# Attention and two mixture layers on one core: a static order planned with later transfers, and one batch's gate logits moved from TensorE to VectorE

## The chip, the cores and the metric

The kernel runs on one core of one Trainium2 chip. A core has five engines that run their own instruction streams and meet at semaphores: TensorE (PE, matmuls; PEld is its weight load), VectorE (DVE), ScalarE (ACT), GpSimd (POOL), and SyncE (SP), which here issues nearly all transfers. The metric is the device time of one execution in microseconds. The kernel before takes 978.87 us, the median of 3 runs (978.06 to 982.78).

## The reference

What is computed, cut to what matters:

```python
def _attn_ref(q, k, v, f):                      # batch 4, heads 8, sequence 576, head size 64
    scores = scale * np.matmul(q, k.transpose(0, 1, 3, 2))
    cum = np.cumsum(np.log(np.clip(f, 0.0001, 1.0)), axis=-1)
    decay = cum[:, :, :, None] - cum[:, :, None, :]
    scores = np.where(causal, -1e9, scores + decay)
    ...                                          # softmax over keys, times v
def _moe_ref(x, w_in, w_out):                    # 2304 tokens, 512 -> 2048 -> 512
    h = np.maximum(x @ w_in, 0.0)
    return h * h @ w_out
def _moe2_ref(x, w_gate, w1, w2):                # 8 experts, 512 -> 1024 -> 512
    cap = N // E                                 # 288 tokens for each expert
    logits = x @ w_gate
    order = np.argsort(-logits.flatten())
    ...                                          # greedy: best pair of token and expert first, while
    ...                                          # the token is free and the expert has room
    for e in range(E):
        mask = assigned == e
        out[mask] = np.maximum(x[mask] @ w1[e], 0.0) @ w2[e]
```

The three stages follow one another: attention gives x, the dense layer gives a new x (called x2 here), and the last layer sends each token of x2 to one expert. The gate's logits are compared exactly, so x2 has to be precise: each matmul of the dense layer is done as three products of high and low parts.

## The kernel before, in words

**The order.** Nothing runs in the order in which the code is written. The code records tasks (class `Sched`, method `op`): what a task reads and writes, which engines can do it (`alts`, with a cost in ns for each), and a priority (`s.base` at the time of recording, then the sequence). `run` then plays all tasks through a list scheduler in its own time: at each moment every free engine takes the ready task of the lowest priority number for which it finds buffers. A task that follows another becomes ready after a latency of the engines involved (`LAT`). For a transfer the plan counts 450 ns of issue, 650 ns of start, its bytes at 310 GB/s on one shared queue, and then 900 ns until it has landed. The result is a fixed order for each engine, and the choice of engine for each task. On the chip each engine takes its instructions strictly in that order and waits in front of one whose inputs are late.

**Attention** works by pairs of heads, four pairs for each of four batches (`pair`, `att_tail`). Queries and keys come by transfers (qk), and the decay of a head comes as a `row` of 128 x 576, a transfer from the scratch `cumd` in DRAM. A mask is added to the row's diagonal block (L512, GpSimd or VectorE), TensorE makes scores (L500), VectorE adds row and scores and takes the minimum in one instruction (L517, statistics in `st`), ScalarE takes the exponential (L524), TensorE transposes it (L556), ScalarE or VectorE copies it out of PSUM (`pa`, `pb`), and TensorE multiplies by v (L573). For the normalisation the sums of a pair get an epsilon (L603) and a reciprocal (L604), are transposed (L606), written to the scratch `rd`, and read back broadcast into the buffer `wraw` (four transfers); the product with them is L622. The result goes to the scratch `xd`.

**Weights of the dense layer** arrive as 64-bit numbers of 512 KB a piece (`w_piece`, into buffers z). VectorE makes 32-bit floats of them in three steps (L652, L653, L654, buffer `wa` or z), ScalarE or GpSimd rounds to the high part (helper lines L384, L386), GpSimd or VectorE subtracts for the low part (L656). The 32 pieces are spread over the attention stage.

**The dense layer** goes by chunks of 256 tokens (`moe1_chunk`): L692 to L694 up, ReLU, square, rounding, low part (L709), L716 to L718 down. As soon as a batch of attention is done its chunks are mixed into the rest of attention.

**The logits** are made in three ways. For batches in `DL` (1 and 2) VectorE multiplies the tile of x2 by each expert's gate column and sums, eight instructions per tile of 128 tokens (`x2_sums`, L797), with the gate columns broadcast in `wgb`. For batch 0, and for one chunk of batch 3, `x2_tail` has TensorE transpose the tile (L822) and multiply by the gate (L830, two passes for 32-bit floats). For the last two chunks of the dense layer the gate is multiplied into w_out beforehand: `gate_weights` does that with 128 instructions like those sums (L852) as filler on VectorE, and TensorE's L758 and L759 use the result. All logits have to be there before routing starts.

**Routing and experts** follow (`phase`, `expert`): routing of expert m overlaps with the matmuls of the experts before it.

Of the kernel before, what the change touches and what calls it, by code (L numbers as in the profile page):

```python
# [8 lines left out]
F = mybir.dt.float32  # L9
R = mybir.dt.float32r  # L10
BF = mybir.dt.bfloat16
# [3 lines left out]
OP = mybir.AluOpType  # L15
# [4 lines left out]
B, H, S, D = 4, 8, 576, 64  # L20
# [5 lines left out]
WHI, WLO = "act pool", "dve pool"  # L26
# [10 lines left out]
HV = [0]  # L37
NSM = 4

DL = (1, 2)  # L40
ABASE = (0, 0.5, 0.6, 2)
HM = 50.0
LM = 40.0
# [24 lines left out]
    "pool": {"pool": 96.0, "dve": 130.0, "act": 130.0, "pe": 230.0, "sp": 150.0},  # L68
}
DMA_GBS = 310.0  # L70
SLOT_LAT = 180.0


# [21 lines left out]


class Task:
    __slots__ = ("alts", "fn", "prio", "deps", "succ", "ready", "bufs", "done", "start", "eng", "nbytes", "seq")


class Sched:
# [31 lines left out]
                o.succ.append(t)  # L133
        return t

    def op(self, alts, fn, r=(), w=(), nbytes=0, prio=None, after=None):
        t = Task()
        t.alts = alts
        t.fn = fn
        t.seq = len(self.tasks)  # L140
        t.prio = (self.base if prio is None else prio, t.seq)
        t.deps, t.succ, t.ready, t.done, t.start, t.eng = set(), [], 0.0, None, None, None
        t.nbytes = nbytes
        t.bufs = []
        if after is not None:
            t.deps.add(after)
        for lst, wr in ((r, False), (w, True)):
            for x in lst:
                b, key = x if isinstance(x, tuple) else (x, None)
                if b not in t.bufs:  # L150
                    t.bufs.append(b)
                    b.left += 1
                    if b.after is not None:
                        t.deps.add(b.after)
                for o, k in b.writers:
                    if o is not t and (k is None or key is None or k == key):
                        t.deps.add(o)
                if wr:
                    for o, k in b.readers:
                        if o is not t and (k is None or key is None or k == key):  # L160
                            t.deps.add(o)
                    b.writers.append((t, key))
                else:
                    b.readers.append((t, key))
        for o in t.deps:
            o.succ.append(t)
        self.tasks.append(t)
        return t

    def run(self):  # L170
# [42 lines left out]
        while ndone < len(self.tasks):  # L213
            progress = True
            while progress:
                progress = False
                for e in list(cand):
                    if busy.get(e, 0.0) > now:
                        continue
                    h = cand[e]  # L220
                    skipped = []
                    pick = None
                    while h:
                        p, t = heapq.heappop(h)
                        if t in started:
                            continue
                        r = t.ready.get(e, 0.0) if isinstance(t.ready, dict) else t.ready
                        if r > now:
                            skipped.append((p, t))
                            continue  # L230
                        sl = can_alloc(t)
                        if sl is None:
                            skipped.append((p, t))
                            continue
                        pick = t
                        break
                    for x in skipped:
                        heapq.heappush(h, x)
                    if pick is None:
                        continue  # L240
                    t = pick
                    sl = can_alloc(t)
                    for b in t.bufs:
                        if b.slots and b.slot is None:
                            b.slot = sl.pop(0)
                            free_slot[b.slot] = 1e18
                            nxt[b.name] += 1
                    started.add(t)
                    t.start, t.eng = now, e
                    order.append(t)  # L250
                    dur = t.alts[e]
                    busy[e] = now + dur
                    fin = now + dur
                    if t.nbytes:
                        st = max(dma_free, fin + 650.0)
                        dma_free = st + t.nbytes / DMA_GBS
                        fin = dma_free + 900.0
                    heapq.heappush(events, (now + dur, cnt, None))
                    cnt += 1
                    heapq.heappush(events, (fin, cnt, t))  # L260
                    cnt += 1
                    progress = True
            if not events:
                left_t = [t for t in self.tasks if t not in started]
                raise RuntimeError(f"static schedule stuck: {len(left_t)} left; first {[(x.alts, x.fn.__qualname__, left[x]) for x in left_t[:8]]}")
            now, _, t = heapq.heappop(events)
            if t is not None:
                t.done = now
                ndone += 1
                for b in t.bufs:  # L270
                    b.left -= 1
                    if b.left == 0 and b.slot is not None:
                        free_slot[b.slot] = now + SLOT_LAT
                        heapq.heappush(events, (now + SLOT_LAT, cnt, None))
                        cnt += 1
                for s in t.succ:
                    left[s] -= 1
                    for e in s.alts:
                        rt = now + LAT.get(t.eng, {}).get(e, 100.0)
                        if not isinstance(s.ready, dict):  # L280
                            s.ready = {}
                        if rt > s.ready.get(e, 0.0):
                            s.ready[e] = rt
                    if left[s] == 0:
                        offer(s)
                        for e in s.alts:
                            heapq.heappush(events, (s.ready[e], cnt, None))
                            cnt += 1
# [33 lines left out]
def dve1(n):  # L322
    return 70 + 1.04 * n
# [46 lines left out]
class K:  # L370
# [269 lines left out]
    def w_piece(self, which, r, c, half, raws, was, hold):  # L640
        s = self.s
        n = 512 if half is None else 256
        o = 256 * half if half else 0
        t, x = self.unit(which, r, c), r % 2
        bh, bl = self.wu[t]
        hi, lo = (lambda: bh[:, x, o:o + n]), (lambda: bl[:, x, o:o + n])
        src = (self.w_in, self.w_out)[which][r * 128:(r + 1) * 128, 512 * c + o:512 * c + o + n]
        raw = s.buf(self.mp, [128, n, 2], U32, "wraw", 0, also=raws)
        a = s.buf(self.mp, [128, n], U32, "wa", 1, also=was)
        self.dma(lambda: raw.t.rearrange("p a b -> p (a b)"), lambda: src.bitcast(U32), 128 * n * 8, w=[raw], after=hold)  # L650

        s.op({"dve": 80 + n}, lambda e: e.tensor_scalar(a.t, raw[:, :, 1], 3, 0x3FFFFFFF, op0=OP.logical_shift_left, op1=OP.bitwise_and), r=[raw], w=[a])  # L652
        s.op({"dve": dve1(n) + 50}, lambda e: e.scalar_tensor_tensor(a.t, raw[:, :, 0], 29, a.t, op0=OP.logical_shift_right, op1=OP.bitwise_or), r=[raw], w=[a])  # L653
        s.op({"dve": dve1(n) + 50}, lambda e: e.scalar_tensor_tensor(a.t, raw[:, :, 1], 0xC0000000, a.t, op0=OP.bitwise_and, op1=OP.bitwise_or), r=[raw], w=[a])  # L654
        s.op(hi_alts(n, WHI), lambda e: self.rnd(e, hi(), a.t.bitcast(F)), r=[a], w=[(bh, x)])
        s.op({"dve": dve1(n) + 300, "pool": ptt(n) + 100}, lambda e: e.tensor_sub(lo(), a.t.bitcast(F), hi().bitcast(F)), r=[a, (bh, x)], w=[(bl, x)])  # L656

    def moe1_x(self, b, c, two=False):
# [130 lines left out]

    def x2_sums(self, b, c, t, acc):  # L790
        s = self.s
        xr = s.buf(self.xp, [128, DM], F, "x2g", 0, also=[("xo", 0), ("xo", 1)])
        xr.after = self.gp.bar
        xr, tt = self.x2_rows(b, c, t, acc, xr)
        for x in range(E):
            jk = s.buf(self.gp, [128, DM], BF, "gjs", 1)
            s.op({"dve": dve1(DM) + 285}, lambda e, x=x, jk=jk: e.tensor_tensor_reduce(  # L797
                out=jk.t, in0=xr.t, in1=self.wgb[:, x, :], scale=1.0, scalar=0.0, op0=OP.mult, op1=OP.add,
                accum_out=self.L[:, tt, x:x + 1]), r=[xr, self.wgb], w=[jk, (self.L, tt)])

    def x2_rows(self, b, c, t, acc, xr=None):
        s, mp = self.s, self.mp
# [629 lines left out]
```

## Time and profile before

| | |
|---|---|
| median of 3 runs | 978.87 us (978.06 to 982.78) |
| the profiled execution | 982.32 us, of which the span from first to last instruction is 980.5 us |
| mean granted TensorE clock | 0.973 of full speed |
| TensorE matmuls / weight loads busy | 930.0 us (95%) / 748.6 us (76%) |
| VectorE / ScalarE / GpSimd busy | 625.1 us (64%) / 396.9 us (40%) / 349.2 us (36%) |
| transfers | 105.66 MB, mean 108 GB/s |

The attention stage, with the first chunks of the dense layer mixed in, lasts to some 296 us; the rest of the dense layer to some 660 us; routing and experts fill the rest. The busy times are means over these stages. Matmuls are pipelined and their ends overlap, so a TensorE that is busy all the time is not yet at its peak rate; the gaps between its instructions, and the granted clock, say more than its share.

### The profile page before, as it was taken

The page shows a single profiled execution, that of the slowest core. Times are in us where ns is not written, and L with a number is a line of the kernel's source. Part 1 is how long each engine was busy: PE and PEld are TensorE (multiplying, and loading weights), DVE is VectorE, ACT ScalarE, POOL GpSimd, SP SyncE. Part 2 cuts the span into 40 slices and gives each one's busy share as a digit, 9 for nine tenths or more (in the row PEclk, how much of TensorE's full clock was granted, in tenths as well). Part 3 has the DMA queues.
Part 4 walks back from the last instruction along what each step waited for, and adds up shares of the span by engine and source line. Part 5 has one row for each costly group of instructions (what it writes and reads, how often), then busy time and mean ns, then how long its engine had stood idle before and what let it go on. Part 6 is the DMA issues. An engine that isn't in the chain of part 4 may idle for free. (4 is left out here: it accounts for less than half of the span.)

```text
span 980.5 us, 17456 instructions
## 1 busy us (share of the span) xinstructions
PE 930.0 (95%) x6135; PEld 748.6 (76%) x6135; DVE 625.1 (64%) x2015; ACT 396.9 (40%) x1079; POOL 349.2 (36%) x470
## 2 busy tenths in 40 slices
PE   6988989999999999999999999995999999999996
PEld 3545556677778898889999899774777877788995
DVE  6978786887544999998536322577767787422231
ACT  4867656756554444444444366100101112224410
POOL 2656454667224323333312100002013032756921
PEclk9998899999999999999999999996999999899999
DMA  6678676543313101011000000037535440434400
GB/s 221 219 227 258 192 234 203 172 153 102 126 51 112 44 1 44 1 44 23 21 23 1 22 1 1 12 97 229 175 133 201 179 156 30 138 116 140 156 25 25
DMA packets 48039, 105.66 MB, mean 108 GB/s; under 512 B 10216, under 2 KB 18568, under 8 KB 47824
## 3 DMA queue, kind: packets, MB, share of 16 engines
q1 hardware_dynamic: 44880, 95.11, 29.9%
q0 software_dynamic: 3072, 9.44, 3.3%
q8 instruction: 48, 0.79, 0.3%
q14 instruction: 39, 0.32, 0.1%
HBM read 90.20 MB, written 14.33 MB: 107 GB/s over the span
## 5 line engine op out<-in xcount | busy, mean ns | idle before, releaser
L692 PE MATMUL u<-xh,z 128*128 128x256 f32 x512 | 149.2, 291 | 0.1
L693 PE MATMUL u<-xh,z 128*128 128x256 f32 x512 | 144.8, 283 | 0.0
L694 PE MATMUL u<-xl,z 128*128 128x256 f32 x512 | 144.8, 283 | 0.0
L697 ACT ACTIVATE r<-u 128x256 f32<-128x256 f32 x144 | 54.7, 380 | 163.4 <-PE u L694 142.8
L709 POOL TENSOR_TENSOR hl<-r,hh 128x256 fp32r<-128x256 f32 x84 | 75.2, 896 | 114.7 <-ACT hh L384 97.1
L852 DVE CUSTOM_DVE_ANT_0 gjk<-wof,wgb 128x512 bf16<-128x512 f32 x128 | 104.7, 818 | 9.9 <-DMA wgb<-wgT 7.4
L692 PEld LDWEIGHTS u<-xh,z 128*128 128x128 f32 x512 | 97.3, 190 | 13.8 <-issue 4.2
L693 PEld LDWEIGHTS u<-xh,z 128*128 128x128 f32 x512 | 97.5, 190 | 7.6
L694 PEld LDWEIGHTS u<-xl,z 128*128 128x128 f32 x512 | 97.4, 190 | 0.0
L1297 PE MATMUL acc<-ehh,z 128*128 128x288 f32 x320 | 91.5, 422 | 0.0
L718 PE MATMUL acc<-z,hl 128*128 128x512 f32 x224 | 88.2, 394 | 1.8 <-POOL hl L709 1.4
L716 PE MATMUL acc<-z,hh 128*128 128x512 f32 x224 | 89.7, 401 | 0.0
L717 PE MATMUL acc<-z,hh 128*128 128x512 f32 x224 | 88.7, 396 | 0.0
L1268 PE MATMUL u<-exh,z 128*128 128x288 f32 x304 | 87.9, 425 | 0.1
L1223 POOL TENSOR_TENSOR z<-wr,z 128x512 fp32r<-128x512 f32 x48 | 60.2, 1287 | 46.6 <-ACT z L384 46.4
L524 ACT ACTIVATE p<-p,st 128x448 f32<-128x448 f32 (+4 forms) x110 | 59.8, 544 | 28.2 <-DVE st L517 27.6
L512 POOL TENSOR_TENSOR row<-maskb,row 128x128 f32<-128x128 bf16 (+1 forms) x97 | 47.9, 498 | 64.7 <-DVE st L517 36.6
L1297 PEld LDWEIGHTS acc<-ehh,z 128*128 128x128 f32 x320 | 58.2, 195 | 15.5 <-issue 1.7
L1268 PEld LDWEIGHTS u<-exh,z 128*128 128x128 f32 x304 | 56.3, 197 | 15.0 <-DVE exh L388 0.3
L1320 POOL DMA_INDIRECT out_dram<-yo,ph_idx x24 | 25.2, 1050 | 100.7 <-DVE yo L388 34.8
L1184 POOL DMA_INDIRECT xg<-x2d,ph_idx x24 | 25.6, 1067 | 96.8 <-DVE ph_eq L1162 51.9
L698 ACT ACTIVATE r<-r 128x256 f32<-128x256 f32 x139 | 58.1, 418 | 4.1
(347 smaller groups left out, 2199.2 us busy)
## 6 DMA issues: line engine op xcount, KB each, us to landing
z<-in_w_dram SPq DMA_DIRECT2D x40, 512.0 KB, 5.1
wr<-in_w_dram SPq DMA_DIRECT2D x24, 512.0 KB, 4.2
z<-in_w_in_dram SPq DMA_DIRECT2D x16, 512.0 KB, 6.6
z<-in_w_out_dram SPq DMA_DIRECT2D x14, 512.0 KB, 4.6
row<-cumd SPq DMA_DIRECT2D x24, 288.0 KB, 6.1
xd<-xo SPq DMA_DIRECT2D x16, 288.0 KB, 2.6
wraw<-rd SPq DMA_DIRECT2D x32, 128.0 KB, 3.0
xa<-xd SPq DMA_DIRECT2D x8, 512.0 KB
```

What stands on the lines that cost most here:

```text
L524: s.op({"act": act(w, extra=2)}, lambda e, x=x, si=si, i=i, n=n, w=w, p=p[x], st=st[x]: e.activation(p[:n, :w], p[:n, :w], AF.Exp, bias=st ...
L692: e.matmul(u[:, :256], wh[:, k % 2, fs], xh[k][1](), start=(k == 0), stop=False)
L693: e.matmul(u[:, :256], wl[:, k % 2, fs], xh[k][1](), start=False, stop=False)
L694: e.matmul(u[:, :256], wh[:, k % 2, fs], xl[k][1](), start=False, stop=(k == 3))
L709: s.op(lo_alts(256), lambda e: e.tensor_sub(hl(), r.t, hh().bitcast(F)), r=[r, kh], w=[kl])
L716: g = [lambda e: e.matmul(acc.t, hh()[:, ts], wh[:, f % 2], start=(f == 0), stop=False), lambda e: e.matmul(acc.t, hh()[:, ts], wl[:, f % ...
L717: lambda e: e.matmul(acc.t, hh()[:, ts], wl[:, f % 2], start=False, stop=False),
L718: lambda e: e.matmul(acc.t, hl()[:, ts], wh[:, f % 2], start=False, stop=(f == 15))]
L852: s.op({"dve": dve1(DM) + 85}, lambda e, f=f, x=x, wo=wo, jk=jk: e.tensor_tensor_reduce(out=jk.t, in0=wo.t, in1=wb[:, x, :], scale=1.0, sc ...
L1223: s.op(lo_alts(512, LOE(m, which, i, 0, c)), lambda e, cs=cs: e.tensor_sub(lo[:, cs], raw[:, cs], hi[:, cs].bitcast(F)), r=[(raw, key), (h ...
L1268: s.op({"pe": 1.69 * CAP}, lambda e, k=k: e.matmul(u[:, :CAP], whi[0][k][:, fs], xh[k].t, start=(k == 0), stop=(k == 3)), r=[(whi[0][k], c ...
L1297: e.matmul(acc[:, :CAP], wh[:, ds], hh.t, start=(f == 0), stop=(f == 7))
```

## The change

Three edits.

1. The plan's constant for the landing of a transfer goes from 900 to 2000 ns (`DMA_LAND`).
2. A task can carry a `lag` that the plan adds to the time at which its successors become ready. The last conversion step of a weight piece (L654 before) gets 1200 ns, the rounding behind it 500 ns. On the chip a lag is nothing; it shapes the order alone.
3. Batch 0 joins `DL`: its four tiles get their logits as sums on VectorE. Since the gate columns `wgb` are not there yet when these tiles are made, `x2_sums` writes the tile to x2d as before, loads it back later into a buffer of its own name (`x2k`, in the same slots xo), at priority 10, and sums with a scratch of its own (`gjk0`).

```diff
-DL = (1, 2)
+DL = (0, 1, 2)
...
+DMA_LAND = 2000.0
 SLOT_LAT = 180.0
...
-                        fin = dma_free + 900.0
+                        fin = dma_free + DMA_LAND
...
-                        rt = now + LAT.get(t.eng, {}).get(e, 100.0)
+                        rt = now + LAT.get(t.eng, {}).get(e, 100.0) + t.lag
...
-        s.op({"dve": dve1(n) + 50}, lambda e: e.scalar_tensor_tensor(a.t, raw[:, :, 1], 0xC0000000, a.t, op0=OP.bitwise_and, op1=OP.bitwise_or), r=[raw], w=[a])
-        s.op(hi_alts(n, WHI), lambda e: self.rnd(e, hi(), a.t.bitcast(F)), r=[a], w=[(bh, x)])
+        s.op({"dve": dve1(n) + 50}, lambda e: e.scalar_tensor_tensor(a.t, raw[:, :, 1], 0xC0000000, a.t, op0=OP.bitwise_and, op1=OP.bitwise_or), r=[raw], w=[a], lag=1200.0)
+        s.op(hi_alts(n, WHI), lambda e: self.rnd(e, hi(), a.t.bitcast(F)), r=[a], w=[(bh, x)], lag=500.0)
...
     def x2_sums(self, b, c, t, acc):
         s = self.s
-        xr = s.buf(self.xp, [128, DM], F, "x2g", 0, also=[("xo", 0), ("xo", 1)])
+        xr = s.buf(self.xp, [128, DM], F, "x2g" if b else "x2k", 0, also=[("xo", 0), ("xo", 1)])
         xr.after = self.gp.bar
-        xr, tt = self.x2_rows(b, c, t, acc, xr)
+        base = s.base
+        if b:
+            xr, tt = self.x2_rows(b, c, t, acc, xr)
+        else:
+
+            _, tt = self.x2_rows(b, c, t, acc)
+            s.base = 10
+            tok = b * S + 64 + c * 256 + t * 128
+            self.dma(lambda: xr.t, lambda: self.x2d[tok:tok + 128, :], 128 * 2048, r=[(self.x2d, tt)], w=[xr])
         for x in range(E):
-            jk = s.buf(self.gp, [128, DM], BF, "gjs", 1)
+            jk = s.buf(self.gp, [128, DM], BF, "gjs" if b else "gjk0", 1)
...
+        s.base = base
```

Since the plan's numbers change, the order changes on every engine, from the first 20 us on. On TensorE the work is the same but for 16 transposes (L822, 24 to 8) and 16 logit products (L830, 24 to 8). On VectorE 32 sums are added. Beside that, tasks change engines: over the whole program the mask addition L512 goes from 121 on GpSimd and 39 on VectorE to 109 and 51, the weights' low part L656 from 29 and 5 to 24 and 10, the dense layer's low part L709 from 85 and 59 to 97 and 47.

Three places in the order follow. The first is SyncE's queue in the attention stage, where the rows for two heads are fetched; z with in_w_in is a weight piece, and the four loads of wraw wait for the landing of the write to rd. Before:

```order
L391 DMA rd<-nrt_952 10x128
L391 DMA z_967<-in_v_dram 128x2x320
L391 DMA wraw_996<-rd 64x64
L391 DMA wraw_996<-rd 64x512
L391 DMA wraw_996<-rd 64x64
L391 DMA wraw_996<-rd 64x512
L391 DMA qk_1036<-in_q_dram 128x576
L391 DMA z_1045<-in_k_dram 128x576
L391 DMA z_1050<-in_w_in_dram 128x1024
L391 DMA row_1069<-cumd 128x576
L391 DMA xd<-xo_923 128x576
L391 DMA row_1099<-cumd 128x576
```

Now, at the same pair (lines stand two further down in the changed file):

```order
L393 DMA rd<-nrt_954 10x128
L393 DMA z_980<-in_v_dram 128x2x320
L393 DMA z_1000<-in_w_in_dram 128x1024
L393 DMA wraw_1015<-rd 64x64
L393 DMA wraw_1015<-rd 64x512
L393 DMA wraw_1015<-rd 64x64
L393 DMA wraw_1015<-rd 64x512
L393 DMA qk_1047<-in_q_dram 128x576
L393 DMA row_1056<-cumd 128x576
L393 DMA row_1067<-cumd 128x576
L393 DMA z_1073<-in_k_dram 128x576
L393 DMA xd<-xo_930 128x576
```

The weight piece moved from between keys and row to ahead of the loads of wraw, both rows follow the queries directly, and the write to xd no longer stands between them.

The second place is VectorE some 50 us into the program, at a pair's normalisation: L622 multiplies one pair's output by wraw, L603 and L604 prepare the sums of the next pair, L653 and L654 are steps of a weight piece. Before:

```order
L517 ISA z_719,st_720<-u_633,row_515 128x512
L517 ISA st_720 128x1
L622 TENSOR_TENSOR xo_553<-xo_553,wraw_656 128x256
L603 TENSOR_SCALAR sums_382<-sums_382 128x10
L653 SCALAR_TENSOR_TENSOR wa_673<-z_416,wa_673 128x512
L604 RECIPROCAL sums_382<-sums_382 128x10
L654 SCALAR_TENSOR_TENSOR wa_673<-z_416,wa_673 128x512
```

Now (L624 is the product with wraw, L605 and L606 are the sums, L654 to L656 the weight steps):

```order
L519 ISA p_712,st_713<-u_629,z_509 128x512
L519 ISA st_713 128x1
L605 TENSOR_SCALAR sums_381<-sums_381 128x10
L656 SCALAR_TENSOR_TENSOR z_617<-z_315,z_617 128x512
L606 RECIPROCAL sums_381<-sums_381 128x10
L654 TENSOR_SCALAR wa_726<-z_367 128x512
L655 SCALAR_TENSOR_TENSOR wa_726<-z_367,wa_726 128x512
L624 TENSOR_TENSOR xo_557<-xo_557,wraw_669 128x256
```

The product with wraw moved behind the sums and three weight steps.

The third place is VectorE behind the end of attention, where the gate weights begin (wof is a row block of w_out put together again, gf collects the gate weights, L the logits). Before:

```order
L849 TENSOR_TENSOR wof_3978<-z_748,z_800 128x512
L622 TENSOR_TENSOR xo_3843<-xo_3843,wraw_3956 128x256
L852 ISA gjk_4104,gf_4105<-wof_3970,wgb_4016 128x512
L852 ISA gf_4105 128x1
L852 ISA gjk_4113,gf_4105<-wof_3970,wgb_4016 128x512
```

Now:

```order
L860 TENSOR_TENSOR wof_3953<-z_833,z_853 128x512
L624 TENSOR_TENSOR xo_3811<-xo_3811,wraw_3931 128x256
L807 ISA gjk_4077,L<-xo_3971,wgb_3977 128x512
L807 ISA L 128x1
L863 ISA gjk_4088,gf_4089<-wof_3945,wgb_3977 128x512
L863 ISA gf_4089 128x1
L807 ISA gjk_4101,L<-xo_3971,wgb_3977 128x512
```

The sums of batch 0 (L807) stand in turn with the gate weights (L863), and go on like that until all 32 are done.

## Rows read from the trace of the kernel before

**Rows 1.** The page: span, and TensorE's and its weight loads' busy time.

```profile
span 980.5 us, 17456 instructions
...
PE 930.0 (95%) x6135; PEld 748.6 (76%) x6135; DVE 625.1 (64%) x2015; ACT 396.9 (40%) x1079; POOL 349.2 (36%) x470
```

**Rows 2.** Busy time by stretch: length, each engine (instructions), granted clock, DMA share, GB/s.

```profile
50.00:75.00 25.00, 21.25 (x150) 11.48 (x145) 19.68 (x67) 17.07 (x54) 13.75 (x23) 1.00 0.68 223
75.00:100.00 25.00, 22.46 (x142) 12.46 (x142) 20.56 (x72) 17.46 (x56) 15.77 (x28) 0.86 0.80 255
100.00:125.00 25.00, 23.17 (x159) 14.02 (x156) 19.87 (x68) 15.33 (x50) 11.57 (x18) 0.86 0.65 203
125.00:150.00 25.00, 22.16 (x139) 13.37 (x138) 19.29 (x56) 12.02 (x39) 14.98 (x21) 0.86 0.78 249
...
250.00:275.00 25.00, 25.00 (x184) 18.26 (x185) 13.37 (x46) 14.11 (x46) 7.99 (x16) 1.00 0.29 96
...
425.00:450.00 25.00, 25.00 (x161) 22.65 (x160) 24.83 (x63) 9.99 (x25) 8.68 (x10) 1.00 0.00 1
```

**Rows 3.** Timeline, 75 to 85 us: start, duration, instruction, [idle before, releaser].

```profile
75.64 0.43 SPq L391 DMA_DIRECT2D z<-in_w_in_dram  x1
...
76.17 0.38 SPq L391 DMA_DIRECT2D row<-cumd  x1
...
82.53 0.81 POOL L512 TENSOR_TENSOR row<-maskb,row 128x128 f32<-128x128 bf16 x2 [4.95 <-DMA row<-cumd]
...
84.06 0.85 PE L500 MATMUL sc<-z,z 64*128 64x192 f32 x6 [1.56 <-DVE st L517]
```

**Rows 4.** Busy time by stretch of 5 us, behind rows 3.

```profile
85.00:90.00 5.00, 5.00 (x23) 3.05 (x22) 3.79 (x7) 3.20 (x9) 4.17 (x7) 0.51 1.07 362
```

**Rows 5.** Timeline, 51 to 54 us.

```profile
51.59 0.43 DVE L622 TENSOR_TENSOR xo<-xo,wraw 128x256 f32<-128x256 f32 x1 [2.05 <-DMA wraw<-rd]
...
53.62 0.27 PE L606 MATMUL pt<-ident,sums 128*10 128x128 f32 x1 [1.50 <-DVE sums L604]
```

**Rows 6.** Waits from 15 to 290 us: us in total, times, longest.

```profile
POOL row L512 <- DMA row<-cumd: 18.2, 10, 4.9
...
DVE xo L622 <- DMA wraw<-rd: 9.7, 9, 2.3
...
ACT z L384 <- DVE wa L654: 6.3, 6, 2.2
...
POOL z L656 <- ACT z L384: 8.0, 7, 2.2
```

**Rows 7.** Timeline of TensorE, 325 to 331 us: logits of two tiles.

```profile
325.77 0.64 PE L822 MATMUL u<-ident,wraw 128*128 128x128 f32 x4
326.17 0.36 PE L692 MATMUL u<-xh,z 128*128 128x256 f32 x1
...
329.14 1.85 PE L830 MATMUL u<-wg,wraw 128*128 128x8 f32 x16
330.85 0.36 PE L692 MATMUL u<-xh,z 128*128 128x256 f32 x1
```

**Rows 8.** Groups by line: count, busy us, mean ns, idle before.

```profile
L797 DVE CUSTOM_DVE_ANT_0 gjs<-xo,wgb 128x512 bf16<-128x512 f32 x64 | 53.2, 832 | 0.9
```

**Rows 9.** One line's instructions: ns min/median/max, first and last start in us.

```profile
L852 DVE CUSTOM_DVE_ANT_0 gjk<-wof,wgb x128: 676/692/1257, 310.4 to 456.9; 128x512 bf16<-128x512 f32 x128
...
L758 PE MATMUL sc<-h,g x8: 280/280/294, 558.4 to 577.1; 128*16 128x256 f32 x8
```

**Rows 10.** Transfers by kind: count, KB each, median us from issue to landing.

```profile
row<-cumd SPq DMA_DIRECT2D x24, 288.0 KB, 6.1
```

**Rows 11.** Groups by line and shape, mask addition and low part on VectorE.

```profile
L512 DVE TENSOR_TENSOR row<-maskb,row 128x128 f32<-128x128 bf16 x27 | 9.8, 368 | 1.9 <-ACT row L384 1.6
...
L656 DVE TENSOR_TENSOR z<-z,z 128x512 fp32r<-128x512 f32 x4 | 4.9, 1228 | 1.4 <-PE ov L573 1.3 <-PE sc L500 0.2
```

**Rows 12.** Timeline of TensorE at the first expert.

```profile
679.29 2.13 PE L1056 MATMUL ov<-ph_G,ph_OH 128*128 128x128 bf16 x18
```

More of the change, by code (lines that the diff above doesn't have):

```diff
@@ L97 @@
 class Task:
-    __slots__ = ("alts", "fn", "prio", "deps", "succ", "ready", "bufs", "done", "start", "eng", "nbytes", "seq")
+    __slots__ = ("alts", "fn", "prio", "deps", "succ", "ready", "bufs", "done", "start", "eng", "nbytes", "seq", "lag")
 class Sched:
@@ L134, in barrier, with op @@
         return t
-    def op(self, alts, fn, r=(), w=(), nbytes=0, prio=None, after=None):
+    def op(self, alts, fn, r=(), w=(), nbytes=0, prio=None, after=None, lag=0.0):
         t = Task()
@@ L143, in op @@
         t.nbytes = nbytes
+        t.lag = lag
         t.bufs = []
```

## Prediction

> **What bounds the kernel now.** I read the page first. The span is 980.5 us and TensorE is busy for 930.0 of it, its weight loads for 748.6 [rows 1]. An average like that hides stages, so I read the table by stretches of 25 us next: it gives busy time and granted clock side by side. From 250 us on TensorE is the bound in the plainest form. At 425 to 450 it is busy for 25.00 of 25 and its weight loads for 22.65; at 250 to 275 also 25.00 [rows 2]. Whatever is taken off TensorE there comes off the time, and whatever VectorE gets there is free while it stays ahead.
>
> Between 50 and 150 us, in the attention stage, it looks different. TensorE is idle for 3.75, 2.54, 1.83 and 2.84 us of the four stretches, 11.0 us in all. In the last three the granted clock is 0.86 on average [rows 2]. A mean of 0.86 between the two levels 2.4 and 1.2 GHz is 28% of 25 us, 7 us, at the lower one, which costs 3.5 us of work: 10.5 us over three stretches. Idle time and clock together are 21.5 us that TensorE could have worked in 100 us. No engine is full there (VectorE 19.3 to 20.6 of 25).
>
> The timeline says what starts such an episode. SyncE issues a 512 KB weight load at 75.64 us and a row of the decay (row<-cumd, 288 KB) behind it at 76.17. GpSimd, which has to add the mask to that row, stands still for 4.95 us until 82.53, VectorE waits for GpSimd, and TensorE's scores start at 84.06 after 1.56 us without work [rows 3]. Right behind that the clock is 0.51, the lower level, through 85 to 90 [rows 4]. A second case: VectorE starts a norm product (L622) at 51.59 after 2.05 us of waiting for the transfer wraw<-rd; the reciprocal of the next pair's sums stands behind it, and TensorE's transpose of these sums begins at 53.62 after 1.50 us of waiting [rows 5]. In both the engine stood in front of an instruction that the plan took to be ready. Summed over 15 to 290 us, GpSimd waited 10 times and 18.2 us for rows, VectorE 9 times and 9.7 us for wraw, ScalarE 6 times and 6.3 us for VectorE's last step of a weight piece (L654), GpSimd 7 times and 8.0 us for ScalarE's rounding before a low part (L656) [rows 6].
>
> **The change part by part.** *TensorE loses four tiles' logits.* In the timeline the four transposes of a tile take from 325.77 to 326.17, 0.40 us; two tiles' logit products take from 329.14 to 330.85, 0.86 us each [rows 7]. That is 1.26 us a tile and 5.0 us for the four tiles of batch 0, on an engine that has no idle time there. The two PSUM banks "u" that the tiles borrowed come free too; I count nothing for it.
>
> *VectorE gains 32 sums.* One takes 832 ns [rows 8], so 32 take 27 us, and with some reads of the accumulator up to 30. They stand in front of and among the gate weights (L852), which now end at 456.9 us, and the first product that uses those is at 558.4 [rows 9]: 101 us of cover for 30 us of delay. If the cover were gone, the last batch's gate products would wait for up to 30 us. What VectorE would otherwise do in that stretch moves to GpSimd (12 more low parts, L709), which is busy for 8.68 of 25 us there [rows 2]; I take nothing. The four loads back from x2d are 1 MB in all, beside the 2 MB load of wgb that VectorE waits for at this place anyway; nothing.
>
> *The plan lets transfers land 1.1 us later* (DMA_LAND). For a row of 288 KB the old plan counts 0.45 + 0.65 + 0.95 + 0.9 = 2.95 us from issue, the new 4.05; the trace has a median of 6.1 us [rows 10], waiting in the queue included (the plan has a queue of its own, so the gap is not all error). The order shows the effect at both cases above: weight loads now stand behind the rows or ahead of the blocked wraw, and L622 stands behind the reciprocal. Where only the slot moves by 1.1 us, a mean row wait of 18.2/10 = 1.82 us keeps 40%, and the wraw wait of 9.7/9 = 1.08 us goes. *The reserves* (1.2 us behind L654, 0.5 us behind the rounding) cover ScalarE's 6.3/6 = 1.05 us whole and 44% of GpSimd's 8.0/7 = 1.14 us. Together 11.0 + 9.7 + 6.3 + 3.5 = 30.5 of the 42.2 us of waits in rows 6, 72%, if nothing new came in their place. Something will: all five engines got a new order. So for TensorE I take half of the 21.5 us, 10.8 us; the bounds are nothing and all of it.
>
> [...]
>
> *VectorE's share in attention grows.* By the count of the two orders, 12 more mask additions (L512, 368 ns) and 5 more low parts (L656, 1228 ns) stand on VectorE instead of GpSimd before the last score: 4.4 + 6.1 = 10.5 us [rows 11]. VectorE has some 5 us free in each 25, so I count nothing; if it were the bound, 10.5 us.
>
> *Later stages.* Ahead of the last attention product the order now has 288 up and 132 down matmuls instead of 291 and 135, at 25/161 = 0.155 us each [rows 2] 0.9 us that moves, not work that is added. At the first expert the second round's histograms (2.13 us at 679.29 [rows 12]) now stand ahead of the transposes of the gathered rows instead of among them. The gathers' landing ends that wait either way, so nothing; at most 2.1 us.
>
> The sum: 5.0 + 10.8 = 15.8 us off the profiled execution, whose span of 980.5 becomes 964.7 and whose own time of 982.3 becomes 966.5. That execution is 3.4 us above the median of the runs, 978.9, so the median becomes **963**.
>
> **The rivals.**
> *New waits take the place of the old.* The order is greedy, and one late row or one weight piece in front of a score costs the same wherever it stands. For it: the new plan's 4.05 us is still below 6.1. Against it: the two cases that I followed are both cleared. Then the 5.0 us of TensorE remain, give or take 2: 972 to 976.
> *Nearly all of attention's loss goes.* For it: the episode of rows 4 starts from a wait of the kind that the change addresses, so shortening a wait can save an episode whole. 5.0 + 21.5 us, up to 2.1 at the gathers: 950 to 956.
> *VectorE becomes the bound of attention.* A low part of 1228 ns ahead of a softmax step (L517) holds up scores, exponentials and transposes. Price 10.5 - 5.0: 5.5 us slower, 984. It decides if VectorE is above some 23 of 25 us between 50 and 200 us. Against it: 19.3 to 20.6 now [rows 2], plus 10.5 spread over some 250 us.
> *The sums change nothing* is a case of the first rival: if TensorE's logits had been hidden behind a wait there, even the 5.0 us would not come; the 25.00 of 25 [rows 2] speak against it.
>
> **How the numbers follow.** Forecast, 957 to 970: 0.46. Nearly all, below 957: 0.13. New waits, 970 to 979: 0.30. VectorE the bound, above 979: 0.11. The range that leaves out 2 in 10 reaches from 952 (a gain of 26.9: TensorE's 5.0 and all of the 21.5) to 977 (a gain of 1.9: TensorE's 5.0 less 3 us of new waits); the likeliest case's own is 957 to 970. A difference of 0.5%, 4.9 us, is about what a measurement of this kernel can tell from none: faster than 974.0 are the first two cases and 0.14 of the third, 0.73; slower than 983.8 is most of the last, 0.09; between them lie 0.18.
>
> **What would show it.** In the profile after: no transposes and logit products of batch 0 between 240 and 340 us; 96 sums on VectorE instead of 64, the gate weights ending near 485 us less what attention saved, and the first gate product not later for it. In the stretches of 25 us from 50 to 150, less than 6 us idle and at most one episode of the lower clock; GpSimd's wait for rows near 7 us, VectorE's for wraw near none, ScalarE's for L654 near none. Wrong it would be if these stretches lose as much as now at other places (the first rival), or if VectorE there is above 23 of 25 us (the third).

## The result, and the profile after

The changed kernel takes 968.22 us (median of 6 runs, 965.04 to 969.91), against 980.27 for the kernel before in the same runs (978.06 to 982.78). The ratio is 0.9873, with a 95% interval of 0.9855 to 0.9891: 1.3% faster. The forecast was 963, the likeliest case's own range 957 to 970.

The page of the changed kernel, which answers to [rows 1]:

```profile
span 965.8 us, 17449 instructions
...
PE 913.3 (95%) x6087; PEld 737.0 (76%) x6087; DVE 658.8 (68%) x2078; ACT 393.4 (41%) x1075; POOL 352.2 (36%) x467
```

Its table by stretches of 25 us, to be laid beside [rows 2] (each engine's busy time, then the granted clock):

```profile
50.00:75.00 25.00, 23.37 (x182) 13.83 (x180) 22.85 (x87) 18.49 (x61) 12.85 (x24) 1.00 0.69 221
75.00:100.00 25.00, 23.26 (x184) 13.98 (x180) 23.75 (x77) 18.84 (x64) 13.86 (x26) 1.00 0.87 274
100.00:125.00 25.00, 22.94 (x154) 14.17 (x154) 22.69 (x70) 16.39 (x51) 15.66 (x26) 0.86 0.66 217
125.00:150.00 25.00, 23.83 (x165) 15.05 (x163) 22.71 (x65) 14.75 (x46) 13.89 (x17) 1.00 0.85 263
150.00:175.00 25.00, 21.61 (x161) 13.90 (x161) 24.18 (x77) 17.62 (x57) 13.73 (x22) 1.00 0.57 177
175.00:200.00 25.00, 24.47 (x166) 17.44 (x166) 24.31 (x53) 17.37 (x49) 16.54 (x17) 1.00 0.57 193
```

The last two of these stretches in the kernel before:

```profile
150.00:175.00 25.00, 24.75 (x173) 16.93 (x173) 18.34 (x61) 18.09 (x56) 11.60 (x21) 1.00 0.54 176
175.00:200.00 25.00, 24.45 (x180) 16.43 (x182) 19.25 (x58) 16.43 (x54) 14.45 (x23) 1.00 0.57 170
```

From 50 to 150 us TensorE is idle for 6.6 us instead of 11.0, and one stretch of the four has the lower clock instead of three: 3.5 us instead of 10.5. From 150 to 175, where it had hardly been idle before, it now is for 3.39 us, and VectorE is busy for 24.18 of 25 there.

The waits from 15 to 290 us answer to [rows 6]; the lines of the code stand two further down:

```profile
POOL xo L624 <- DMA wraw<-rd: 19.5, 10, 4.2
POOL row L514 <- DMA row<-cumd: 13.5, 13, 3.1
...
DVE xo L624 <- DMA wraw<-rd: 6.2, 3, 4.1
...
ACT z L386 <- DVE z L656: 5.7, 5, 2.9
...
ACT z L386 <- DVE wa L656: 0.9, 1, 0.9
```

GpSimd's wait for rows fell from 18.2 to 13.5 us, VectorE's for wraw from 9.7 to 6.2, and ScalarE's for the last step of a weight piece in `wa` from 6.3 to 0.9 (for pieces in z it went from 3.7 to 5.7). GpSimd takes part of the products with wraw too, and its own wait for that transfer, which is not in [rows 6], rose to the 19.5 us above; before it was:

```profile
POOL xo L622 <- DMA wraw<-rd: 12.8, 6, 3.6
```

Later on, what was forecast for the sums and the gate weights stands in three lines (one line's instructions, as in [rows 9]):

```profile
L807 DVE CUSTOM_DVE_ANT_0 gjk<-xo,wgb x32: 676/682/1268, 296.6 to 347.4; 128x512 bf16<-128x512 f32 x32
L863 DVE CUSTOM_DVE_ANT_0 gjk<-wof,wgb x128: 678/691/1279, 297.2 to 480.9; 128x512 bf16<-128x512 f32 x128
...
L760 PE MATMUL sc<-h,g x8: 279/280/293, 545.1 to 563.8; 128*16 128x256 f32 x8
```

Batch 0's 32 sums run from 296.6 to 347.4 us, the gate weights end at 480.9, and the first product with them starts at 545.1, 13.3 us earlier than before. The cover held.

One more line says how far the dense layer is: the start of its last up matmul on xh (L694, before L692), called the last up matmul below. Before, and in the changed kernel:

```profile
L692 PE MATMUL u<-xh,z x512: 274/283/580, 132.0 to 615.1; 128*128 128x256 f32 x171
...
L694 PE MATMUL u<-xh,z x512: 275/283/388, 122.5 to 601.7; 128*128 128x256 f32 x171
```

So 13.4 of the 14.7 us by which the span is shorter were gained by then. What lies behind, routing and experts, is 365.4 us before and 364.1 after; it is not part of the question.

### The profile page after: what moved, and what is told of

Read it like the earlier page. It is cut to its first block, busy times and chain, and to the rows that moved or that the text cites. A ratio compares the mean times of both kernels' runs of the same rounds, so it can differ in the third digit from the quotient of the medians.

```text
span 965.8 us, 17449 instructions
## 1 busy us (share of the span) xinstructions
PE 913.3 (95%) x6087; PEld 737.0 (76%) x6087; DVE 658.8 (68%) x2078; ACT 393.4 (41%) x1075; POOL 352.2 (36%) x467
## 5 line engine op out<-in xcount | busy, mean ns | idle before, releaser
L694 PE MATMUL u<-xh,z 128*128 128x256 f32 x512 | 148.9, 291 | 0.4 <-ACT r L699 0.3
L711 POOL TENSOR_TENSOR hl<-r,hh 128x256 fp32r<-128x256 f32 x96 | 88.7, 926 | 132.3 <-ACT hh L386 116.9
L863 DVE CUSTOM_DVE_ANT_0 gjk<-wof,wgb 128x512 bf16<-128x512 f32 x128 | 109.0, 852 | 1.4
L694 PEld LDWEIGHTS u<-xh,z 128*128 128x128 f32 x512 | 97.2, 190 | 13.2 <-issue 3.4
L1308 PE MATMUL acc<-ehh,z 128*128 128x288 f32 x320 | 89.0, 413 | 0.0
L514 POOL TENSOR_TENSOR row<-maskb,row 128x128 f32<-128x128 bf16 (+1 forms) x90 | 44.3, 497 | 74.6 <-DVE st L519 57.6
L1331 POOL DMA_INDIRECT out_dram<-yo,ph_idx x24 | 24.3, 1011 | 100.3 <-DVE ph_P L1097 32.3
```

Source lines behind the costliest of these rows:

```text
L694: e.matmul(u[:, :256], wh[:, k % 2, fs], xh[k][1](), start=(k == 0), stop=False)
L711: s.op(lo_alts(256), lambda e: e.tensor_sub(hl(), r.t, hh().bitcast(F)), r=[r, kh], w=[kl])
L863: s.op({"dve": dve1(DM) + 85}, lambda e, f=f, x=x, wo=wo, jk=jk: e.tensor_tensor_reduce(out=jk.t, in0=wo.t, in1=wb[:, x, :], scale=1.0, sc ...
L1308: e.matmul(acc[:, :CAP], wh[:, ds], hh.t, start=(f == 0), stop=(f == 7))
```

## The experiments

Twelve kernels were run, each against the kernel before on the same chip.

**One part alone.** Four kernels: the sums alone, both planning edits, the landing constant alone, the reserves alone.

```diff
# sums_only: the changed kernel with
DMA_LAND = 900.0      lag=0.0 and lag=0.0
# order_only: DL = (1, 2)
# land_only:  DL = (1, 2)   lag=0.0 and lag=0.0
# lag_only:   DL = (1, 2)   DMA_LAND = 900.0
```

> The kernel before with batch 0 in DL alone; the plan's numbers stay as they were, so attention's order hardly changes. If TensorE's work that is taken away is what counts (the prediction's first term): 5.0 us less than before, 0.995. If new waits for GpSimd's low part, as seen in the changed kernel between 300 and 550 us, take back what is saved: 2 to 4 us less, 0.996 to 0.998. If VectorE's sums made attention or the gate products late: not faster than before.

> Both planning edits, the logits of batch 0 left on TensorE. If the parts add, what is left of the measured 12 us after the sums' 3 to 5: 7 to 9 us less than before, 0.991 to 0.993, with one episode of the lower clock in attention instead of three. If the order is a matter of luck, any time from 972 to 985 us, since this order is not the one of the changed kernel either.

> Only the landing constant, 900 to 2000 ns. By the reasons of the prediction it owns 7.3 of row waits and 9.7 of wraw waits, 17 of the 30.5 us of waits that the edits cover, so somewhat more than half of what both planning edits give: 4 to 6 us less than before, 0.994 to 0.996, and VectorE's wait for wraw near none. If the order is a matter of luck, the time has no relation to that: within 6 us of before on either side.

> Only the reserves behind the weight conversion and the rounding. By the reasons of the prediction they cover 6.3 us of ScalarE's and 3.5 us of GpSimd's waits, and TensorE gets the smaller part: 2 to 4 us less than before, 0.996 to 0.998, and ScalarE's wait for VectorE's last conversion step falls from 6.3 to 1 us or less. If the order is a matter of luck: within 6 us of before on either side.

Measured, with 95% intervals: sums alone 1.0003 (0.9978 to 1.0028), both planning edits 0.9924 (0.9894 to 0.9955), the landing constant 0.9909 (0.9885 to 0.9934), the reserves 1.0120 (1.0093 to 1.0147). The landing constant gives all that the two planning edits give, and 4 to 6 us was too little for it. The reserves, from which 2 to 4 us were expected, cost 12 us when they stand alone, although they do what they were costed for. The waits of their kernel from 15 to 290 us:

```profile
POOL row L514 <- DMA row<-cumd: 16.7, 8, 4.5
...
DVE xo L624 <- DMA wraw<-rd: 16.1, 12, 2.5
...
ACT z L386 <- DVE wa L656: 1.2, 2, 0.9
```

ScalarE's wait is gone (6.3 to 1.2), but VectorE now stands before wraw for 16.1 us instead of 9.7. A reserve shifts the whole order, and here the products with wraw met transfers that were later still.

**What does a new order do by itself, and which transfer carries the landing constant?** Four kernels: one neutral number of the plan, and the 2000 ns for one kind of transfer at a time.

```diff
# nudge_before, in the kernel before
-SLOT_LAT = 180.0
+SLOT_LAT = 190.0
# rows_late, wraw_late, weights_late: the changed kernel with DL = (1, 2)   lag=0.0 and lag=0.0
# and a mark "late" for tasks
-DMA_LAND = 2000.0
+DMA_LAND = 900.0
+LATE = 2000.0
...
-                        fin = dma_free + DMA_LAND
+                        fin = dma_free + (LATE if t.late else DMA_LAND)
# late=True for: the rows from cumd | the write to rd and the loads of wraw | the 512 KB weight pieces
```

> The kernel before with one number of the plan changed that no row of its profile asks for: the time after which a freed buffer counts as free, 180 to 190 ns. It moves as many rows of the order as the landing constant does. If the time follows from the reasons (later transfers, fewer waits), this gives no change: 0.995 to 1.005. If any new order rolls the dice, it lands anywhere between the 0.991 of the landing constant alone and the 1.012 of the reserves alone.

> The kernel before, with 2000 ns of landing for the 24 row loads from cumd alone, 900 ns for all other transfers. If the gain of the landing constant comes from the rows: near its 0.991, 0.990 to 0.994, and GpSimd's wait for rows falls from 18.2 us to 10 or less. If it comes from wraw or the weights, or from the order as a whole: 0.996 to 1.004.

> The same for the write to rd and the loads of wraw behind it alone, two landings in a row, so 2.2 us more before the product L622. If the prediction's second case carries the gain: VectorE's wait for wraw falls from 9.7 us to 2 or less and the time to 0.993 to 0.996. If VectorE's product only moves and GpSimd's rows stay late: 0.998 to 1.004.

> The same for the 512 KB weight pieces alone. By the prediction's reasons these loads are no cause of a wait of their own: 0.997 to 1.003. If delaying the weights in the plan costs as the reserves did (their kernel starts the dense layer at 176.6 instead of 132.0 us and is 1.2% slower): 1.003 to 1.012.

Measured: the nudge 1.0058 (1.0034 to 1.0082), rows late 1.0079 (1.0049 to 1.0109), wraw late 0.9919 (0.9898 to 0.9940), weights late 1.0041 (1.0013 to 1.0069). So a new order by itself does move the time, by 0.6% here. Rows late and weights late are not told apart from such a nudge; wraw late is, and lies on the other side of 1. Rows, of whose waits the prediction took 11.0 us as covered (the expectation above names 7.3, the part that it took to remain), give nothing although their wait is all but removed; in the kernel with the rows late:

```profile
POOL row L516 <- DMA row<-cumd: 2.4, 4, 1.4
...
DVE xo L626 <- DMA wraw<-rd: 12.3, 9, 2.0
```

and in the one with wraw late:

```profile
POOL row L516 <- DMA row<-cumd: 12.7, 9, 3.2
...
DVE xo L626 <- DMA wraw<-rd: 5.0, 3, 3.1
```

GpSimd's wait for rows fell from 18.2 to 2.4 us in the kernel that became slower; the one with 12.7 us of it is faster by the whole gain of the landing constant.

**Is it VectorE's stand in front of the product with wraw?** Two kernels take that product off VectorE, one takes the landing constant away from wraw alone, one leaves the reserves out.

```diff
# norm_pool (in the kernel before), norm_pool_after (in the changed kernel)
-            s.op({"dve": dve1(n) + 200, "pool": ptt(n) + 200}, lambda e, c0=c0, c1=c1: e.tensor_mul(xo...
+            s.op({"pool": ptt(n) + 200}, lambda e, c0=c0, c1=c1: e.tensor_mul(xo...
# wraw_early (in the changed kernel), soon=True for the write to rd and the loads of wraw
-                        fin = dma_free + DMA_LAND
+                        fin = dma_free + (900.0 if t.soon else DMA_LAND)
# land_sums (in the changed kernel): lag=0.0 and lag=0.0
```

> The kernel before with the product L622 on GpSimd alone, landing constant 900 as before. In the eight kernels measured so far those whose VectorE waits 6.2 us or less for wraw are 0.8 to 1.3% faster, those where it waits 9.7 us or more are not faster. If VectorE's stand in front of that product is the cause, it is gone here by construction: 0.990 to 0.994, although GpSimd waits for wraw longer than before. If the sorting by that wait is an accident of eight orders: 0.996 to 1.010, as for the other kernels that keep 900 ns.

> The changed kernel with 900 ns again for the write to rd and the loads of wraw alone; 2000 ns for all else, reserves and sums kept. If wraw is what the landing constant gives: VectorE waits for wraw 10 us or more again and the kernel loses most of its gain, 0.995 to 1.003. If the gain lies in rows or in the rest: 0.986 to 0.991.

> The changed kernel without the reserves. The landing constant alone was 0.991 and both planning edits 0.992; if the reserves give nothing and the sums give TensorE's 5.0 us in this order too: 0.985 to 0.988, as the changed kernel or a little faster. If the reserves are needed: 0.991 or more.

> The changed kernel with the product with wraw on GpSimd alone. If VectorE's wait for wraw is the cause, the 6.2 us of it that are left go too: 0.980 to 0.985, the fastest so far. If GpSimd, with 17 more products and longer waits, makes mask additions and low parts late: 0.988 to 0.995.

Measured: the product on GpSimd in the kernel before 1.0036 (1.0005 to 1.0066), wraw early in the changed kernel 1.0091 (1.0057 to 1.0126), the changed kernel without reserves 0.9823 (0.9785 to 0.9861), the product on GpSimd in the changed kernel 0.9864 (0.9825 to 0.9902). In the second, with 900 ns for these five transfers of a pair and 2000 ns for all others, the gain is gone, and more. That kernel keeps the reserves, which alone cost as much (1.0120); what all other transfers late would give without the reserves was not run. Taken together the ratios sort without an exception: the six kernels whose plan has 2000 ns for this chain are at 0.9924 or less, and the eight with 900 ns, the kernel before among them, at 1 or more. The first and the last speak against the simple form of the mechanism: VectorE no longer waits for wraw at all there, and yet the one gains nothing and the other no more than the change itself. In the kernel before with the product on GpSimd, that engine waits instead (from 15 to 290 us):

```profile
POOL row L512 <- DVE st L517: 28.3, 24, 4.0
POOL xo L622 <- DMA wraw<-rd: 27.7, 14, 5.4
POOL row L512 <- DMA row<-cumd: 15.6, 15, 3.9
```

It stands before wraw for 27.7 us instead of 12.8, with the next masks of rows queued behind. The version without the reserves is the fastest run here, 962.43 us (959.51 to 964.05). Its interval and that of the change, measured at another time, just touch.

**One account for all fourteen.** From the stretches of each profiled execution (25 us from 50 to 200, else 50 or 100) I add up what TensorE lost up to 600 us: idle time, and for the clock (1 - granted clock) x length, as the prediction did. "Rest" is the start of the last up matmul less that loss.

| kernel | ratio | last up matmul | idle to 300 | clock | idle 300 to 600 | loss | rest | VectorE waits for wraw | VectorE busy 50 to 200 |
|---|---|---|---|---|---|---|---|---|---|
| before | 1 | 615.1 | 21.5 | 10.5 | 2.7 | 34.6 | 580.5 | 9.7 | 117.0 |
| nudge_before | 1.0058 | 619.5 | 26.2 | 11.8 | 2.4 | 40.4 | 579.1 | 14.9 | 126.9 |
| norm_pool | 1.0036 | 612.4 | 24.8 | 3.5 | 3.9 | 32.2 | 580.2 | 0 | 130.7 |
| lag_only | 1.0120 | 627.7 | 30.0 | 10.5 | 4.5 | 45.0 | 582.7 | 16.1 | 122.5 |
| rows_late | 1.0079 | 626.2 | 25.9 | 15.5 | 4.8 | 46.2 | 580.0 | 12.3 | 117.9 |
| weights_late | 1.0041 | 617.9 | 22.8 | 8.5 | 4.8 | 36.0 | 581.9 | 15.4 | 119.7 |
| wraw_late | 0.9919 | 609.0 | 18.6 | 5.2 | 3.6 | 27.4 | 581.6 | 5.0 | 131.8 |
| order_only | 0.9924 | 605.8 | 19.8 | 0 | 4.6 | 24.3 | 581.5 | 5.1 | 141.7 |
| land_only | 0.9909 | 603.3 | 16.6 | 1.7 | 3.7 | 22.0 | 581.3 | 6.0 | 142.2 |
| sums_only | 1.0003 | 615.2 | 25.4 | 11.8 | 4.0 | 41.1 | 574.1 | 10.6 | 119.9 |
| wraw_early | 1.0091 | 621.7 | 27.8 | 15.2 | 5.2 | 48.2 | 573.5 | 12.1 | 128.3 |
| norm_pool_after | 0.9864 | 601.6 | 18.8 | 8.2 | 2.7 | 29.7 | 571.9 | 0 | 136.1 |
| after | 0.9873 | 601.7 | 20.7 | 3.5 | 4.1 | 28.4 | 573.3 | 6.2 | 140.5 |
| land_sums | 0.9823 | 597.3 | 18.9 | 1.5 | 2.9 | 23.3 | 574.0 | 7.9 | 141.5 |

The rest is 579.1 to 582.7 in the nine kernels that leave batch 0's logits on TensorE, and 571.9 to 574.1 in the five that don't. Two numbers therefore tell when the dense layer ends: TensorE's work, and what it loses in waits and clock, between 22 and 48 us. In these executions the order shows in the second alone. Each row is a single execution, while the ratio is that of medians: those of nudge_before, lag_only and rows_late took 5 to 6 us longer than their kernels' medians, that of norm_pool 2.9 us less, so a few us between two rows say little.

## Why the prediction was right, and where not

**What bounds the kernel.** Right. In these executions the end of the dense layer moves with TensorE's loss, most of it in attention, and with TensorE's work, and the loss is idle time and lower clock together. Of the clock's part the changed kernel keeps one episode. It begins as those before did, behind a wait. In the timeline, three instructions and then TensorE's scores:

```profile
99.08 0.16 DVE L605 TENSOR_SCALAR sums<-sums 128x10 f32<-128x10 f32 x1
...
101.88 1.32 POOL L658 TENSOR_TENSOR z<-wa,z 128x512 fp32r<-128x512 f32 x1
101.99 1.35 DVE L514 TENSOR_TENSOR z<-maskb,z 128x128 f32<-128x128 bf16 x1
...
103.94 1.40 PE L502 MATMUL sc<-z,qk 64*128 64x192 f32 x8 [2.06 <-DVE st L519]
```

A mask addition (L514) on VectorE takes 1.35 us beside GpSimd's low part, the sums of row and score behind it are late, and TensorE's scores with them, after 2.06 us without work. The next 5 us are near the lower level (0.56 of full speed):

```profile
105.00:110.00 5.00, 5.00 (x27) 3.13 (x27) 2.85 (x8) 2.40 (x8) 1.96 (x4) 0.56 0.51 150
```

**TensorE's logits, -5.0 us.** Borne out with the landing constant in the plan, not without it: 0.9873 with them gone and 0.9924 without is a ratio of 0.9949, 5.0 us, and without the reserves 0.9823 to 0.9909 is 8.5 us. The intervals leave some 3.5 and 4.4 us either way, so that the first is just 5.0 is luck. The rest in the table is lower by 5.0 us between the two groups' nearest members and by 7.6 in the mean (581.0 and 573.4); the 5.0 were read from rows, and where more would come from stays open. Alone, the sums gave nothing (1.0003), against the expectation of 5.0. Their order is the kernel before's on every engine up to 249 us, and in the profiled execution this part lost more all the same (75 to 100 us, as in [rows 2]):

```profile
75.00:100.00 25.00, 18.40 (x113) 11.19 (x114) 20.75 (x64) 15.86 (x51) 14.86 (x25) 0.90 0.72 231
```

TensorE is busy for 18.40 us against 22.46 and gets through 113 instructions against 142, of the same sequence. Up to there it is a difference between two executions of one order: the same instruction of TensorE starts at 248.9 us before and at 251.5 here. From there to the last up matmul this kernel gains 2.5 us. Why the medians show no gain either, over 12 runs, is not settled.

**The attention stage, -10.8 us.** Right in its place, too large in size. Between 50 and 150 us the loss fell from 21.5 to 10.1, by 11.4. But from 150 to 200 it rose by 3.1 (0.80 to 3.92 of idle time), so that up to 300 us 7.7 are left of it, and 1.5 more go between 300 and 600, where TensorE waits longer for GpSimd's low part. The waits from 300 to 620 us, before and after:

```profile
PE acc L718 <- POOL hl L709: 1.1, 3, 0.7
...
PE acc L720 <- POOL hl L711: 2.6, 4, 0.7
```

Over the dense layer's whole length the loss fell from 34.6 to 28.4, by 6.2. That is the mis-sized term: 6.2 instead of 10.8. With the 5.0 it makes 11.2 of the 13.4 us that were measured there. The 10.8 were half of what attention lost, and no row gives the half; that the sum came out as near as it did is in part luck. Of the signs that were named, the single episode of the lower clock and ScalarE's wait (0.9 us) came; idle time was 6.6 us and not less than 6, GpSimd's wait for rows 13.5 and not near 7, VectorE's for wraw 6.2 and not near none.

**Where these microseconds come from.** This step failed. "Together 30.5 of the 42.2 us of waits, 72%" gave each wait a share by its length, 11.0 us to the rows, 9.7 to wraw, 9.8 to the reserves. The runs put the gain at wraw: late for wraw alone 0.9919, late for everything but wraw 1.0091 (reserves and sums kept), rows alone 1.0079, reserves alone 1.0120, and without them the changed kernel is at 0.9823. A wait's length was no measure of its worth: rows lost 15.8 us of waits and the kernel became no faster. The list was not whole either: it leaves out GpSimd's 12.8 us for wraw, and in the changed kernel both engines together wait longer for wraw than before (25.7 against 22.5 us).

**What is it about wraw?** Among the kernels that leave the product on both engines, those whose VectorE waits 7.9 us or less for wraw are faster, those with 9.7 or more are not (one execution of each). But a cause would have to act when it is taken away by other means, and with the product on GpSimd alone it didn't. Shown is that the plan's landing for this chain decides between gain and none; that VectorE's stand is how it acts is not, and how it does act stays open. GpSimd's stand isn't simply the other half: it waits 27.7 us for wraw in norm_pool, which gains nothing, and 32.0 in land_sums, the fastest. Which instruction behind the product has to be late for TensorE to lose, the totals by line don't say.

**New waits take the place of the old (0.30).** In part true: the 3.1 us from 150 to 200 and the 1.5 behind 300 are new ones, and they are most of what the forecast was short by.

**VectorE as the bound (0.11).** The size of its growth came out by luck: by the 50 us stretches up to 300 it goes from 219.4 to 235.4 us, of which some 3.4 are the first sums and gate weights behind 296, so 12.6 against 10.5. But up to 290 us the mask additions on VectorE (L514, before L512) grew by 10.3 us (14.8 to 25.1) where 4.4 were counted, and the low parts (L658, before L656) by 1.3 (5.9 to 7.2) where 6.1 were. The deciding point, "above some 23 of 25 us", was wrong: VectorE is above it at 75 to 100 and from 150 to 200, and the kernel is faster. Between 150 and 200, though, this rival's mechanism is there: TensorE waits for VectorE's copies (L390) for 2.8 us, where before it waited for VectorE for 0.3. The waits of that stretch, before and in the changed kernel:

```profile
PE sc L500 <- DVE st L517: 0.3, 1, 0.3
...
PE ov L558 <- DVE xo L390: 1.2, 1, 1.2
...
PE ov L575 <- DVE pa L390: 0.6, 1, 0.6
PE ov L558 <- DVE pa L390: 0.5, 1, 0.5
PE pt L558 <- DVE pa L390: 0.5, 1, 0.5
```

These new waits were outweighed, not absent. The last column of the table is 131.8 to 142.2 in the kernels that gained and 117.0 to 130.7 in those that didn't, so a full VectorE in a fixed stretch doesn't by itself tell a kernel that is held up from one that gets on faster.

**The sums under cover, and the experts.** Right: 96 sums, the gate weights end at 480.9 us (485 less the saving was said), and their first product is not late. The histograms at the first expert cost nothing that can be seen. One sum of the range is off by a little: 5.0 and 21.5 are 26.5, not 26.9; nothing hangs on it.

## What to carry to other kernels

Take the worth of a wait from what the bounding engine loses behind it, not from its length: here 16 us of waits for one kind of transfer were worth nothing, and 5 us less in front of another came with the whole gain of the landing constant. When an edit changes the plan of a scheduler, run its parts one at a time and a neutral nudge beside them; the nudge alone moved this kernel by 0.6%, one half of the planning edit lost 1.2% by itself, and leaving it out gave the fastest version. And sum idle time and lost clock on the bounding engine stage by stage: that account closed to within 2 us of its group's mean for fourteen kernels.

## What the runs showed of the hardware

Some short instructions of VectorE took several times as long when they began while an operation with two inputs ran on GpSimd. In the timeline above the mask addition of 101.99 us takes 1.35 us, beside a low part on GpSimd from 101.88 to 103.20; at 165.44 us of the same trace the same kind of addition takes 0.29. The epsilon on the sums took 0.16 us at 99.08 and here 0.83:

```profile
161.28 1.02 POOL L624 TENSOR_TENSOR xo<-xo,wraw 128x320 f32<-128x320 f32 x1 [0.24 <-PE ov L558]
161.50 0.83 DVE L605 TENSOR_SCALAR sums<-sums 128x10 f32<-128x10 f32 x1
...
165.44 0.29 DVE L514 TENSOR_TENSOR row<-maskb,row 128x128 f32<-128x128 bf16 x1
```

Each ends within 0.15 us of GpSimd's instruction. In the fourteen traces together 275 of the 558 mask additions of 128x128 on VectorE began beside such an operation; their median is 511 ns, that of the others 286. For the epsilon on the sums (10 numbers in each partition) it is 637 ns for 88 of 224, against 167 for the others. The reciprocal of the same 10 numbers takes 207 ns beside GpSimd's operations and 208 without them.

The Trainium skill (SBUF — State Buffer, "SBUF: two separate sides") says that VectorE, in an instruction with two inputs in SBUF or in a mode that uses two ports, shares a pair of ports with GpSimd, and that the instruction that starts first has the pair for its whole length. The mask additions, with two inputs, agree with that in the median of 511 ns; whether the epsilon, with one input, runs in such a mode, no run here shows.

A mask addition on VectorE thus cost more than the 368 ns of [rows 11]. Up to 290 us 23 of 41 began beside such an operation on GpSimd, instead of 16 of 33, and took 674 ns in the mean, instead of 477. For those on a row alone:

```profile
L514 DVE TENSOR_TENSOR row<-maskb,row 128x128 f32<-128x128 bf16 x33 | 16.7, 510 | 1.9 <-ACT row L386 1.6
```

Executions of one program differed by far more than expected: the kernel before took between 973.9 and 988.1 us in 23 runs, while the kernels that gained stayed within 4 to 9 us, though in 6 or 7 runs only.
